# Attention and a gated layer on one core: three pairs of transposes cut into 64-row halves, an earlier release of the weight loads, and a new order of the instructions

## The chip, the core and the metric

The kernel runs on one core of a Trainium2 chip. The core has five engines that each work through a queue of their own: TensorE (PE; its weight loads are listed as PEld), VectorE (DVE), ScalarE (ACT), GpSimd (POOL) and SyncE (SP), which here only issues transfers (DMAs). Engines wait for each other through semaphores. The metric is the time of one execution on the device in microseconds (us); lower is better.

## The reference

The input `x` has 2048 rows of 448 features. Two layers follow each other, each on a normalized copy of its input and added to it:

```
xn  = layernorm(x)
q, k, v = split(xn @ wqkv)                 # 16 heads of 28
phi(t)  = [softmax(t @ w_phi), softmax(-t @ w_phi)]          # per head, 56 features
kv = phi(k)^T v ;  z = sum over rows of phi(k)               # per head, over all 2048 rows
o  = phi(q) kv / (phi(q) z + 1e-6)
h  = x + o @ wo
hn = layernorm(h)
out = h + (sigmoid(hn @ w_gate) * (hn @ w_up)) @ w_down      # 1792 inner features
```

All tensors are bf16. `kv` and `z` need every row before the first row of `o` can be made.

## The kernel before

**Tiles and stages.** The 2048 rows are 16 tiles of 128, in four chunks of four tiles. First stage: per tile `t` the statistics (`bst`, `agg`, `pow1`, `nm1`), the normalized tile `xn`, its transpose `xT` (features on partitions), then the projections. `Wk` and `Wq` are folded with `w_phi` first (`wT`, `w2m`, `w2e`). Tiles 0 to 3 are projected in pairs (`vv` for v, `pp` for the k features), tiles 4 to 15 one by one (`pva`, `pvb`, which make both). From a tile's projections come the copy of v (`v1`), two exponentials (`ek`), their sums and reciprocals (`ss`, `rs`), the features `phi`, and the kv product `kva`, `kvb`, summed in PSUM over all tiles. `pq` makes the q features of a chunk, `eq` their exponentials. Second stage: `kvz` takes the kv sums out of PSUM, and per tile `num` multiplies, `rsm qq b c rden o` divide (in `o` the tile is ready), `oT` transposes, `woa`/`wob` project, and `h` adds the residual. Third stage: layernorm of `h` (`nm sq ve pow2 hn`, for tiles 0 and 1 `bs2 ag2 pow2 hn`), its transpose `hT`, the gate and up matmuls (`ga`, `gb`), the sigmoid (`sig`) and the product (`hh`), the down matmuls (`dn`, `dp`, `dm`, `dl`), the last addition (`fin`) and `out`. Names end in the tile, or in the first tile and a part.

**64-row halves.** The 448 features of a contraction are laid out so that every matmul uses only 64 rows of the array, and two matmuls, on the upper and the lower 64 rows, run side by side into two PSUM banks (`pair` and `both`, L304 to L325, which call the matmul at L309). The second half of such a pair (`pvb`, `ppb`, `gb`...) exchanges the banks of the first, so each bank is written from the other half of the array; `op` is told which half writes which bank (`half`), and where that changes (`crosses`, L74) PE waits for its own earlier matmuls.

**Transposes.** Those of `xT4` to `xT15`, and of `oT` and `hT` from tile 2 on, are transposing transfers issued by SP (L583, L823, L856). The first ones, `xT0` to `xT3`, `oT0 oT1`, `hT0 hT1`, are made on PE by `pe_transpose` (L533): four transposes of 128 x 128 with all 128 rows into one bank, and one copy out of it by ACT or DVE (`evac`, L529), whose name ends in `e` (`xT2e`). `oT0` and `hT0` are called by `otrans` (L817) and `htrans` (L859).

**What sets the order.** `ORDER` (L223) lists every instruction group by name for each of the five queues; the engine on which a name stands is the engine that does it, where a choice exists. `Graph` (L19) keeps for each tile of memory who wrote and read it last and emits the waits. Two names, `wwo` and `wgu`, emit nothing but waits on PE: for the loads of `wo`, and for those of the gate and up weights. `PACE` (L289) adds one wait to SP's queue: the load `ld_wg1` waits for a kv product; all later loads and transposing transfers are queued behind it. The waits that the prediction speaks of: `ppa2` (tiles 2 and 3) needs both transposes, and its banks emptied by `ek0` and `ek1`; `pva4` needs `v1_2` and `ek2`; `pqa2_1` needs the banks of `pqa1_1` emptied by two `eq`; `num2` and later products write the banks that `c` of the tile before reads; `woa0` needs both `oT` and the banks they were copied from; `ga0_2` needs both `hT`, and `ga0_0` the bank that `eq3_1` empties.

Of the kernel before, what the change touches and what calls it, by code (L numbers as in the profile page):

```python
# [18 lines left out]
class Graph:  # L19
# [90 lines left out]
    def emit(self, nc):  # L110
# [85 lines left out]
P = 128  # L196
# [92 lines left out]
PACE = {"ld_wg1": "kva14"}  # L289
# [36 lines left out]
def build(nc, A_x, A_wqkv, A_w_phi, A_wo, B_w_gate, B_w_up, B_w_down, out):  # L326
# [10 lines left out]
    with ExitStack() as es:  # L337
# [71 lines left out]
        def B(i):  # L409
            return ("bank", i)  # L410
# [121 lines left out]

        def pe_transpose(name, srcs, bank, dst, rkey, wkey):  # L533
            ps = bk16(bank)[:, 0:512]

            def f(e):
                for kt, src in enumerate(srcs):
                    p = e.transpose(ps[:, kt * P:(kt + 1) * P], src, ident[:])  # L538
# [25 lines left out]
        def xnorm(t, a):  # L564
# [14 lines left out]
            if t < 4:  # L579
                pe_transpose("xT%d" % t, [xn_pad[:, s, kt * P:(kt + 1) * P] for kt in range(KT)], 6 + t % 2,  # L580
                             xnT[0][:, :, TS(t)], ("xn", s), ("xnT", t))
            else:
                op("sp", "xT%d" % t, lambda e: e.dma_start_transpose(out=xnT[t // 4][:, :, TS(t)], in_=xn_pad[:, s, :]),  # L583
                   r=[("xn", s)], w=[("xnT", t)], dma="tr", nring=64)
# [67 lines left out]
        def proj(t):  # L652
            bp, bv = t % 2, 2 + t % 2
            pairop("pva%d" % t, "pvb%d" % t, pair(bk(bp)[:, 0:D], bk(bv)[:, 0:D], x(t), x(t), wk2, wv),
                   [("xnT", t)] + W2k + wv_keys, bp, bv)

        def proj2(nm, t, b, w, r):
            pairop("%sa%d" % (nm, t), "%sb%d" % (nm, t), pair(bk(b)[:, 0:D], bk(b + 1)[:, 0:D], x(t), x(t + 1), w, w),
                   [("xnT", t), ("xnT", t + 1)] + r, b, b + 1)
# [51 lines left out]
        def pq(c, i, b):  # L711
# [3 lines left out]
            r = W2q + [("xnT", 4 * c + j) for j in range(4)]  # L715
# [101 lines left out]
        def otrans(t):  # L817
            so = t % NO
            if t < 2:
                pe_transpose("oT%d" % t, [o_pad[:, so, kt * P:(kt + 1) * P] for kt in range(KT)], 2 + t % 2, oT[:, so, :, :],  # L820
                             ("opad", so), ("oT", so))
            else:
                op("sp", "oT%d" % t, lambda e: e.dma_start_transpose(out=oT[:, so, :, :], in_=o_pad[:, so, :]),  # L823
                   r=[("opad", so)], w=[("oT", so)], dma="tr", nring=64)

        def resid(t, b, ha=False):
# [28 lines left out]
            if t >= 2:  # L855
                op("sp", "hT%d" % t, lambda e: e.dma_start_transpose(out=hnT[c][:, :, TS(t)], in_=hn_pad[:, s, :]),  # L856
                   r=[("hn", s)], w=[("xnT", t)], dma="tr", nring=64)

        def htrans(t):  # L859
            s = t % NH  # L860
            pe_transpose("hT%d" % t, [hn_pad[:, s, kt * P:(kt + 1) * P] for kt in range(KT)], t, hnT[0][:, :, TS(t)], ("hn", s), ("xnT", t))

        def wout(t):
# [14 lines left out]
            r = [("oT", t % NO), ("oT", (t + 1) % NO)] + wo_keys + ([("x", t), ("x", t + 1), "ident"] if ha else [])  # L878
# [5 lines left out]
        def wout1(t):  # L884
# [5 lines left out]
            r = [("oT", so)] + wo_keys  # L890
# [10 lines left out]
        def gate_up(t0, n, ff):  # L901
# [3 lines left out]
            hk = [("xnT", t) for t in range(t0, t0 + n)]  # L905
# [129 lines left out]
```

## Time and profile before

| | us |
|---|---|
| median of 3 runs | 202.55 |
| the three runs | 202.16 to 202.61 |
| the profiled execution, its own time | 202.7 |
| its span in the profile | 200.8 |
| PE busy in the span | 195.5 |
| DVE busy | 132.0 |
| ACT busy | 89.4 |
| POOL busy | 56.2 |

The profile is one execution; times in it start with its span, which leaves out 1.9 us around it. "Busy" of PE includes the tail of every matmul, so a busy PE can still be standing between two starts; starts in the timeline show that better. The page's chain goes back from the last instruction to what released it each time. In the timeline a row gives start, length, engine, line and operation, what is written and read, how many instructions are merged in it, and in brackets how long the engine had stood and for whom. Because a helper records all paired matmuls, their line is L309 for all of them, and they are told apart by what they read: `Wk`/`wv_sb` with `xnT` is `pva`/`pvb`, `Wq` is `pq`, `v,phi` is a kv product, `kvz,eq` is `num`, `wg_sb`/`wu_sb` is `ga`/`gb`, `wo_e`/`wo_o` is `woa`/`wob`. L538 is a transpose on PE, L612 a fold (`w2m`), L671/L672 are the two exponentials of `ek`, L721 one of `eq`.

### The profile page before, as it was taken

How to read it: one execution, taken by the hardware profiler on the slowest of the kernel's cores; microseconds unless marked ns; L12 is line 12 of the kernel's file. 1: busy time of each engine (PE TensorE's matmuls, PEld its weight loads, DVE VectorE, ACT ScalarE, POOL GpSimd, SP SyncE). 2: the span in 40 equal slices, each digit the busy share in tenths (PEclk: the TensorE clock that was granted, in tenths of full speed). 3: DMA queues.
4: the chain of work that ended last, by engine and by line, in shares of the span. 5: the costliest groups of instructions: out<-in, count | busy, mean ns of one | idle time of the engine just before them, and what ended most of it. 6: DMA issues, size and time to landing. Idle time of an engine off the chain costs nothing.

```text
span 200.8 us, 5854 instructions
## 1 busy us (share of the span) xinstructions
PE 195.5 (97%) x2516; PEld 114.4 (57%) x2516; DVE 132.0 (66%) x308; ACT 89.4 (45%) x174; POOL 56.2 (28%) x95
## 2 busy tenths in 40 slices
PE   7999999999999999999999999999999999999995
PEld 4835556565568778787444444555555555554443
DVE  5999999978888986576569877346332422272224
ACT  2668988898883451434232432324323212222220
POOL 5779948633343207510170110001400000000000
PEclk9999999999999999999999999999999999999999
DMA  6965346749984230360015220020312000004002
GB/s 157 316 140 129 54 83 76 221 144 302 309 206 66 52 57 15 66 82 3 0 29 124 56 42 10 20 58 26 65 38 52 0 3 2 0 3 137 0 3 91
DMA packets 32490, 16.26 MB, mean 81 GB/s; under 512 B 24720, under 2 KB 31568, under 8 KB 32464
## 3 DMA queue, kind: packets, MB, share of 16 engines
q1 hardware_dynamic: 32336, 15.86, 33.7%
q8 instruction: 20, 0.33, 0.7%
q14 instruction: 6, 0.05, 0.1%
q10 hardware_dynamic: 128, 0.03, 0.1%
HBM read 8.34 MB, written 1.84 MB: 51 GB/s over the span
## 4 chain that ended last, share of the span: by engine, by line
PE 92%; ACT 3%; DMA 2%; issue 1%; SPq 1%; DVE 0%
PE psum L309 84%; PE psum L954 5%; DMA wk_sb<-in_A_wqkv_dram 2%; ACT hhT L671 1%; ACT eq L721 1%; ACT hhT L672 1%; PE psum L524 1%; PE psum L538 1%; PE psum L612 1%; SPq L413 1%; PE psum L599 0%; ACT xnT L531 0%; ACT v L531 0%; DVE x_sb L961 0%
## 5 line engine op out<-in xcount | busy, mean ns | idle before, releaser
L309 PE MATMUL psum<-xnT,wu_sb 64*128 64x512 bf16 (+1 forms) x490 | 93.6, 333 | 0.0
L309 PE MATMUL psum<-xnT,wg_sb 64*128 64x512 bf16 (+1 forms) x490 | 93.5, 333 | 0.1
L925 ACT ACTIVATE sg_sb<-psum 128x512 bf16<-128x512 f32 x56 | 33.2, 596 | 90.1 <-PE psum L309 89.5
L926 DVE SCALAR_TENSOR_TENSOR hhT<-sg_sb,psum 128x512 bf16<-128x512 bf16 x56 | 37.7, 684 | 52.1 <-ACT sg_sb L925 51.7
L309 PEld LDWEIGHTS psum<-xnT,wg_sb 64*128 64x128 bf16 x490 | 44.6, 94 | 20.9 <-DVE hhT L926 2.5
L309 PEld LDWEIGHTS psum<-xnT,wu_sb 64*128 64x128 bf16 x490 | 44.7, 94 | 13.9
L309 PE MATMUL psum<-wd_sb,hhT 64*128 64x448 bf16 x336 | 37.3, 349 | 0.0
L309 PEld LDWEIGHTS psum<-wd_sb,hhT 64*128 64x128 bf16 x336 | 17.8, 94 | 14.2 <-DVE x_sb L836 0.5
L309 PE MATMUL psum<-Wk,xnT 64*128 64x448 bf16 x112 | 22.2, 350 | 0.5 <-ACT hhT L672 0.2
L309 PE MATMUL psum<-wv_sb,xnT 64*128 64x448 bf16 x112 | 22.3, 351 | 0.1
L810 POOL TENSOR_TENSOR o_pad<-c_sb,rden 128x448 bf16<-128x448 bf16 x11 | 10.2, 935 | 28.5 <-DVE rden L806 28.4
L675 DVE TENSOR_REDUCE ss<-hhT 128x32 f32<-128x896 bf16 x16 | 16.8, 1060 | 0.2 <-ACT hhT L672 0.2
L721 ACT ACTIVATE eq<-psum 120x1024 bf16<-120x1024 f32 x16 | 15.6, 1030 | 0.6 <-PE psum L309 0.4
L685 POOL TENSOR_TENSOR phi<-hhT,rs 128x896 bf16<-128x896 bf16 x8 | 13.6, 1710 | 5.6 <-DVE rs L681 3.4
L309 PE MATMUL psum<-xnT,Wq 64*120 64x512 bf16 x112 | 14.8, 383 | 0.3 <-ACT eq L721 0.2
L845 POOL TENSOR_SCALAR ve<-ssq 128x1 f32<-128x1 f32 x11 | 2.2, 201 | 41.8 <-ACT junk L842 41.5
L309 PE MATMUL psum<-wo_o,oT 64*128 64x448 bf16 x56 | 13.2, 350 | 0.0
L309 PE MATMUL psum<-wo_e,oT 64*128 64x448 bf16 x56 | 13.2, 349 | 0.0
L961 DVE SCALAR_TENSOR_TENSOR x_sb<-psum,x_sb 128x448 bf16<-128x448 f32 (+2 forms) x17 | 9.4, 592 | 2.9 <-PE psum L954 1.6
L954 PE MATMUL psum<-wd_sb,hhT 128*128 128x448 bf16 (+2 forms) x70 | 11.2, 316 | 0.0
L309 PEld LDWEIGHTS psum<-Wk,xnT 64*128 64x128 bf16 x112 | 7.8, 94 | 5.8 <-PE psum L309 1.0
L671 ACT ACTIVATE hhT<-psum 128x448 bf16<-128x448 f32 x16 | 8.8, 553 | 4.4 <-PE psum L309 4.2
(105 smaller groups left out, 234.4 us busy)
## 6 DMA issues: line engine op xcount, KB each, us to landing
out_dram<-x_sb SPq DMA_DIRECT2D x15, 112.0 KB, 1.8
x_sb<-in_A_x_dram SPq DMA_DIRECT2D x7, 224.0 KB, 4.2
wd_sb<-in_B_w_down_dram SPq DMA_DIRECT2D x7, 224.0 KB, 5.1
wg_sb<-in_B_w_gate_dram SPq DMA_DIRECT2D x3, 448.0 KB, 5.8
wu_sb<-in_B_w_up_dram SPq DMA_DIRECT2D x3, 448.0 KB, 5.7
wv_sb<-in_A_wqkv_dram SPq DMA_DIRECT2D x2, 224.0 KB, 4.7
wk_sb<-in_A_wqkv_dram SPq DMA_DIRECT2D x2, 196.0 KB, 4.1
wo_e<-in_A_wo_dram SPq DMA_DIRECT2D x1, 336.0 KB, 3.3
```

The lines of the kernel that those rows point to most:

```text
L309: p = e.matmul(o, lhsT=w, rhs=r, start=st, stop=sp, tile_position=(row, 0))
L413: return op(eng, name, lambda e: e.dma_start(dst, src), r=r, w=w, dma="in" if eng == "sp" else "ain", nring=48 if eng == "sp" else 8, kb=kb)
L671: e.activation(ek[:, s, :, 0, :], src, ACT.Exp)
L675: op("dve", "ss%d" % t, lambda e: e.tensor_reduce(ss[:, s, :].rearrange("p (b h) -> p b h", h=2), eks.rearrange("p b (d h) -> p b h d", h= ...
L685: return e.tensor_tensor(phi[:, sp, :, :, :].rearrange("p b a n -> p (b a) n")[:, :, 0:56].rearrange("p b (d h) -> p b d h", h=2), eks.rea ...
L721: op("act", "eq%d_%d%s" % (c, i, "pm"[sg]), lambda e, sg=sg: e.activation(eq[c][:, sg, 2 * i:2 * i + 2, :].rearrange("p g n -> p (g n)"), ...
L810: return e.tensor_tensor(o_pad[:, t % NO, off:off + D].rearrange("p (h d) -> p h d", h=H), c_sb[:, t % NS, :, 0:DH], rden[:, t % NS, :][:, ...
L845: op(("pool", "dve"), "ve%d" % t, lambda e: e.tensor_scalar(ve2[:, t:t + 1], ssq2[:, t:t + 1], 1.0 / D ** 3, EPS, op0=ALU.mult, op1=ALU.ad ...
L925: op("act", "sig" + nm, lambda e: e.activation(sg_sb[:, k, 0:W], bk(bg)[:, 0:W], ACT.Tanh, scale=0.5), r=[B(bg)], w=[("sg", k)])
L926: op("dve", "hh" + nm, lambda e: e.scalar_tensor_tensor(out=dst, in0=sg_sb[:, k, 0:W].rearrange("p (f n) -> p f n", n=N), scalar=1.0, in1= ...
L954: p = e.matmul(bk(b)[:, lo:hi], lhsT=hb[:, ff, TS(t)], rhs=wd_sb[:, ff, lo:hi], start=ff == 0, stop=ff == FT - 1)
L961: op("dve", "fin%d%s" % (t, nm), lambda e: e.scalar_tensor_tensor(out=h_sb[:, t, lo:hi], in0=bk(b)[:, lo:hi], scalar=0.5, in1=h_sb[:, t, l ...
```

## The change

Three pairs of PE transposes (`xT2 xT3`, `oT0 oT1`, `hT0 hT1`) become one group each, made by a new helper: every 128 x 128 transpose is cut into its upper and lower 64 rows, at the row halves 0 and 64 of the array, like the matmuls around it. The upper halves of both tiles go to one bank and the lower halves to the other, and one copy per bank writes that half of both tiles:

```
+        def pair_transpose(names, srcs, banks, dst, rkeys, wkeys):
+            ps = [bk16(b)[:, 0:512] for b in banks]
+
+            def f(e):
+                for i, tile in enumerate(srcs):
+                    for kt, src in enumerate(tile):
+                        o = slice((i * KT + kt) * 64, (i * KT + kt + 1) * 64)
+                        for h, rows in enumerate((LO, HI)):
+                            p = e.transpose(ps[h][:, o], src[rows], ident[rows, rows], tile_position=(64 * h, 0))
+                return p
+            op("pe", names[0], f, r=["ident"] + rkeys, w=[B(b) for b in banks], rows=64, half={b: h for h, b in enumerate(banks)})
+            for h in range(2):
+                evac(names[h] + "e", dst[h], ps[h].rearrange("p (t k s) -> p t k s", t=2, k=KT), B(banks[h]), [k[h] for k in wkeys])
...
-            if t < 4:
+            if t in (2, 3):
...
-PACE = {"ld_wg1": "kva14"}
+PACE = {"ld_wg1": "kva12"}
```

So a reader of either tile waits for both copies. `otrans` and `htrans` call the helper once, for tiles 0 and 1 together. The release of `ld_wg1` and of what SP has behind it moves from the kv product of tile 14 to that of tile 12.

The four orders of ACT, PE, DVE and POOL are new (SP's is the same). Where the prediction speaks of them, first as before and then as after:

```
PE   ppa0 ppb0 warm9 xT2 xT3 vva0 vvb0 ppa2 ppb2 vva2 seed vvb2 w2m1_0 w2m1_1 kva0 pva4 kvb0 pvb4 pva5 w2m1_2 w2m1_3 pvb5
     ppa0 warm9 ppb0 vva0 xT2 vvb0 ppa2 seed ppb2 vva2 w2m1_1 vvb2 w2m1_0 w2m1_3 kva0 pva4 pvb4 pva5 kvb0 kva1 pvb5 w2m1_2
PE   qs pqa1_1 num0 num1 pqb1_1 pqa2_0 num2 pqb2_0 pqa2_1 oT0 oT1 num3 pqb2_1 woa0 wob0 pqa3_0 num4
     qs pqa1_1 num0 pqb1_1 num1 pqa2_0 num2 pqb2_0 pqa2_1 oT0 pqb2_1 num3 woa0 wob0 pqa3_0 wgu num4
PE   pqb3_0 pqa3_1 pqb3_1 num5 hT1 hT0 woa2 ga0_2 ga0_0 ga0_1 num6
     pqb3_0 pqa3_1 pqb3_1 num5 hT0 woa2 ga0_2 ga0_0 ga0_1 num6
PE   woa4 num8 wob4 ga0_8 ga0_9 ga0_10 gb0_8 gb0_9 woa6 ga0_11 wob6 gb0_10 ga0_12 gb0_11 ga0_13 dn0_0 dn0_4 gb0_12 gb0_13 num9
     woa4 num8 wob4 ga0_8 ga0_9 ga0_10 ga0_11 gb0_8 gb0_9 gb0_10 woa6 num9 wob6 ga0_12 ga0_13 gb0_11 wwo gb0_12 gb0_13 dn0_0 dn0_4 dn0_8
ACT  w2e0_2 par ek0 xT3e ek1 v1_0 v1_1 nm1_6 ek2 ek3 v1_2
     w2e0_2 nm1_4 par ek0 ek1 v1_1 nm1_6 v1_0 ek2 w2e1_1 v1_2 ek3
ACT  eq1_0p kvzA kvzB eq1_0m eq1_1p eq1_1m eq2_0m oT0e eq2_0p eq2_1m eq2_1p h1 h0 eq3_0p eq3_0m eq3_1p eq3_1m
     eq1_0m kvzB kvzA eq1_0p eq1_1m eq1_1p eq2_0p oT1e oT0e eq2_0m eq2_1p eq2_1m h0 h1 eq3_0m eq3_0p eq3_1p eq3_1m
DVE  bst4 xn2 agg5 agg4 agg7 bst6 xT2e agg6 ss0
     bst4 agg5 agg4 agg7 xn2 bst6 bst9 xT3e xT2e agg6 ss0
DVE  c1 rsm2 rden1 qq2 b2 c2 oT1e rsm3 rden2
     c1 rsm2 rden1 qq2 o1 b2 c2 rden2 rsm3
DVE  o7 hh0_4 ve3 hh0_6 h4 nm2 h5 nm3 rsm8 hn2 hn3 qq8 hh0_8 h6 h7 b8 c8 rden8
     o7 hh0_4 hh0_6 rsm8 qq8 h5 h4 b8 c8 nm4 rden8 hh0_8 h6 h7
POOL o4 o5 o6 ve2 pow2_2 pow2_3 ve5
     o4 o5 o6 nm3 nm2 ve2 pow2_2 hn2 ve3 pow2_3 hn3 ve4
```

`phi5` and `phi11` move from DVE to POOL and `phi10` the other way, `v1_13` from DVE to ACT, `o1` from POOL to DVE. From `ga4_1` (the gate matmuls of the second chunk) on, PE's order is the same as before but for `dp2_0`, one place earlier, and the moved `wgu`.

More of the change, by code (lines that the diff above doesn't have):

```diff
@@ L578, in xnorm @@
             op(("act", "dve", "pool"), "xn%d" % t, (fa, fd, fp), r=[("x", t), ("rst1", a), need], w=[("xn", s)])
-            if t < 4:
+            if t in (2, 3):
+                if t == 3:
+                    v = xnT[0][:, :, 2 * P:4 * P].rearrange("p k (t h s) -> p h t k s", t=2, h=2)
+                    pair_transpose(("xT2", "xT3"), [[xn_pad[:, u % NX, kt * P:(kt + 1) * P] for kt in range(KT)] for u in (2, 3)], (6, 7),
+                                   [v[:, 0], v[:, 1]], [("xn", 2 % NX), ("xn", 3 % NX)], [XT(2), XT(3)])
+            elif t < 2:
                 pe_transpose("xT%d" % t, [xn_pad[:, s, kt * P:(kt + 1) * P] for kt in range(KT)], 6 + t % 2,
-                             xnT[0][:, :, TS(t)], ("xn", s), ("xnT", t))
+                             xnT[0][:, :, TS(t)], ("xn", s), XT(t))
             else:
                 op("sp", "xT%d" % t, lambda e: e.dma_start_transpose(out=xnT[t // 4][:, :, TS(t)], in_=xn_pad[:, s, :]),
-                   r=[("xn", s)], w=[("xnT", t)], dma="tr", nring=64)
+                   r=[("xn", s)], w=[XT(t)], dma="tr", nring=64)
         for ts in ([0], [1], [2], [3], [4, 5], [6, 7], [8, 9, 10, 11], [12, 13, 14, 15]):
@@ L714, in pq @@
                           lambda h, k: xnT[c][h, k, :], lambda h, k: xnT[c][h, k, :])
-            r = W2q + [("xnT", 4 * c + j) for j in range(4)]
+            r = W2q + [XT(4 * c + j) for j in range(4)]
             op("pe", "pqa%d_%d" % (c, i), f1, r=r, w=[B(b), B(b + 1)], rows=64, half={b: 0, b + 1: 1})
@@ L819, in otrans @@
             if t < 2:
-                pe_transpose("oT%d" % t, [o_pad[:, so, kt * P:(kt + 1) * P] for kt in range(KT)], 2 + t % 2, oT[:, so, :, :],
-                             ("opad", so), ("oT", so))
+                if t == 1:
+                    v = oT[:, 0:2, :, :].rearrange("p t k (h s) -> p h t k s", h=2)
+                    pair_transpose(("oT0", "oT1"), [[o_pad[:, u, kt * P:(kt + 1) * P] for kt in range(KT)] for u in (0, 1)], (2, 3),
+                                   [v[:, 0], v[:, 1]], [("opad", 0), ("opad", 1)], [OT(0), OT(1)])
             else:
                 op("sp", "oT%d" % t, lambda e: e.dma_start_transpose(out=oT[:, so, :, :], in_=o_pad[:, so, :]),
-                   r=[("opad", so)], w=[("oT", so)], dma="tr", nring=64)
+                   r=[("opad", so)], w=[OT(so)], dma="tr", nring=64)
         def resid(t, b, ha=False):
@@ L856, in resid @@
                 op("sp", "hT%d" % t, lambda e: e.dma_start_transpose(out=hnT[c][:, :, TS(t)], in_=hn_pad[:, s, :]),
-                   r=[("hn", s)], w=[("xnT", t)], dma="tr", nring=64)
+                   r=[("hn", s)], w=[XT(t)], dma="tr", nring=64)
         def htrans(t):
-            s = t % NH
-            pe_transpose("hT%d" % t, [hn_pad[:, s, kt * P:(kt + 1) * P] for kt in range(KT)], t, hnT[0][:, :, TS(t)], ("hn", s), ("xnT", t))
+            if t == 1:
+                v = hnT[0][:, :, 0:2 * P].rearrange("p k (t h s) -> p h t k s", t=2, h=2)
+                pair_transpose(("hT0", "hT1"), [[hn_pad[:, u, kt * P:(kt + 1) * P] for kt in range(KT)] for u in (0, 1)], (0, 1),
+                               [v[:, 0], v[:, 1]], [("hn", 0), ("hn", 1)], [XT(0), XT(1)])
         def wout(t):
@@ L877, in fb @@
                             xp(t, 2, HI, False) + [(bk(2)[:, 0:D], ot(t)(HI, k), wo_e[HI, k, :], False, k == 2) for k in (0, 1, 2)])
-            r = [("oT", t % NO), ("oT", (t + 1) % NO)] + wo_keys + ([("x", t), ("x", t + 1), "ident"] if ha else [])
+            r = [OT(t % NO), OT((t + 1) % NO)] + wo_keys + ([("x", t), ("x", t + 1), "ident"] if ha else [])
             op("pe", "woa%d" % t, fa, r=r, w=[B(2), B(3)], rows=64, half={2: 0, 3: 1})
@@ L889, in part @@
                 return [(bk(b)[:, 0:D], oT[h, so, k, :], w[h, k, :], first and k == ks[0], not first and k == ks[-1]) for k in ks]
[L890 removed]
+            r = [OT(so)] + wo_keys
             op("pe", "woa%d" % t, lambda e: both(e, part(LO, lo, True), []), r=r, w=[B(b)], rows=64, half={b: 0})
@@ L904, in gate_up @@
             ns = slice((t0 % 4) * P, (t0 % 4) * P + N)
-            hk = [("xnT", t) for t in range(t0, t0 + n)]
+            hk = [XT(t) for t in range(t0, t0 + n)]
             two = n == 2
```

8 lines of the change are left out of this document (6 added, 2 removed), and 64 rows, old and new, of the table ORDER.

## The prediction

> **What bounds the kernel now.** I read the page first: busy shares, the slices, and the chain that ended last.
>
> ```profile
> span 200.8 us, 5854 instructions
> PE 195.5 (97%) x2516; PEld 114.4 (57%) x2516; DVE 132.0 (66%) x308; ACT 89.4 (45%) x174; POOL 56.2 (28%) x95
> ...
> PEclk9999999999999999999999999999999999999999
> ...
> PE 92%; ACT 3%; DMA 2%; issue 1%; SPq 1%; DVE 0%
> ```
>
> TensorE (PE) holds 92% of the chain, at full granted clock in every slice. The change adds no matmul columns, so the answer lies in the small rest: where PE stands. For that I read the same chain in order of time (start, length, what).
>
> ```profile
> 10.55 0.76 PE psum L309 x6
> ...
> 11.34 0.54 ACT hhT L671
> 11.88 0.43 ACT hhT L672
> 12.32 0.48 ACT xnT L531
> 12.79 0.45 ACT hhT L671
> 13.24 0.45 ACT hhT L672
> ...
> 13.82 0.95 PE psum L309 x8
> ...
> 18.02 2.49 PE psum L309 x30
> 20.52 0.50 PE psum L612 x8
> ...
> 47.20 1.95 ACT eq L721 x2
> ...
> 58.21 65.46 PE psum L309 x960
> ```
>
> The reader is to see two things. ACT sets the pace from 11.34 to 13.69 (`ek0`, the copy `xT3e`, `ek1`) and from 47.20 to 49.15 (`eq1_1p`, `eq1_1m`). From 58.21 on the chain is PE for 65 us without a break: whatever PE wins before that point is kept, if nothing new stops it later. Times below are on the axis of this execution; an earlier start is written as a shift.
>
> **Part 1: the transposes themselves.** Rows of the PE timeline, from `num0` to `num3`:
>
> ```profile
> 45.86 0.63 PE L309 MATMUL psum<-kvz,eq 56*128 56x60 bf16 x32
> 46.31 1.72 PE L309 MATMUL psum<-xnT,Wq 64*120 64x512 bf16 x14
> ...
> 49.19 1.07 PE L309 MATMUL psum<-xnT,Wq 64*120 64x512 bf16 x8 [0.25 <-ACT eq L721]
> 50.20 0.62 PE L538 MATMUL psum<-ident,o_pad 128*128 128x128 bf16 x8
> 50.75 0.40 PE L309 MATMUL psum<-kvz,eq 56*128 56x60 bf16 x16
> ```
>
> Eight 128-row transposes (`oT0 oT1`) hold PE from 50.20 to 50.75, 0.55 us. Some 0.1 of it is the switch back to 64-row work, and I put as much for the switch ahead of 50.20 (an estimate: the row shows only its sum with the matmuls). The new pair has 16 pieces of 64 columns, in two row halves side by side, without a switch. The nearest row is 32 matmuls of 60 columns from 45.86 to 46.31: 14 ns apart, so 16 take 0.23. A pair saves 0.55 + 0.1 - 0.23 = 0.42, and three pairs 1.26. That is the naive sum. I don't forecast it, because at all three places PE stands for something else just before or behind. Bounds for a pair: -0.42 if the halves overlap as in that row, -0.20 if they don't (16 x 28 ns = 0.45).
>
> The Trainium skill ("TensorE: Matmul & The Clock Gate", Part 1, under "Wait — 56ns, not 53.3ns?") speaks against small pieces: starts of matmuls are never closer than about 25 ns, however few columns they have. By it a pair would take 16 x 25 = 0.40 us and save 0.25. The row above has 14 ns over both halves together, so the measurement decides here, and the floor can hold at most for one half by itself.
>
> **Part 2: the start, to `pva4`.** In the chain above `ek0`, `xT3e`, `ek1` follow on ACT and `ppa2` starts at 13.82, when `ek1` has emptied its bank. The change moves `xT3e` to VectorE (DVE): 0.48 leaves ACT's chain. Into ACT's queue comes `nm1_4`, with `par` and `ek0` queued behind its wait for `agg4` and `agg5`, which DVE now does before `xn2`.
>
> ```profile
> 10.63 0.40 DVE L573 TENSOR_SCALAR xn_pad<-x_sb,mv,rst 128x512 bf16<-128x512 bf16 x1
> 10.95 0.33 DVE L546 BATCH_NORM_AGGREGATE mv<-st 128x2 f32<-128x9 f32 x3
> ...
> 11.78 0.42 DVE L531 COPY xnT<-psum 128x512 bf16<-128x512 bf16 x1
> ```
>
> Moved ahead of `xn2` the three aggregates end near 10.95, so `nm1_4` is done by 11.2, and `ek0`, which waits for `ppb0` until 11.31, loses nothing. `ppb0` itself comes 0.06 later, since `warm9` with two switches now stands between `ppa0` and `ppb0`. So `ek1` ends at 13.69 - 0.48 + 0.06 = 13.27. The other input of `ppa2` is the pair's copies, both on DVE: the pair runs behind `vva0` at about 11.95, and two copies of 0.42 end near 13.15. ACT stays last: `ppa2` at 13.40, -0.42. `pva4` (18.02) keeps that: its releasers `ek2` and `v1_2` follow PE, and `v1_2` has one Wq copy ahead of it in place of `ek3`. Bounds: 0 (if the copies, in a DVE queue that is full here, come last) and -0.60.
>
> **Part 3: tiles 4 to 15, to the kv sums.** PE is full here but for small stands between `pva` and `pvb`, which exchange banks:
>
> ```profile
> 26.26 0.28 PE L309 MATMUL psum<-v,phi 64*128 64x58 bf16 x8
> 26.49 0.36 PE L309 MATMUL psum<-wv_sb,xnT 64*128 64x448 bf16 x1
> ...
> 30.18 0.39 PE L309 MATMUL psum<-v,phi 64*128 64x58 bf16 x16
> 30.41 0.36 PE L309 MATMUL psum<-wv_sb,xnT 64*128 64x448 bf16 x1
> ```
>
> Between the start of the kv products and the first `pvb` matmul lie 0.23 us, whether one product (8 matmuls, half of it) or two (16) are put there: one leaves 0.12 unused, two nothing. Before, six tiles have one (4, 8, 9, 11, 13, 14). After, five have one (6, 8, 9, 11, 14) and one has none (`pva4 pvb4`): -0.12 + 0.23. `w2m1_3`, nearly half of the 0.50 at 20.52, leaves this stretch for the one before, where ACT is last: -0.21. Sum -0.10. DVE gives `phi5` to POOL and `v1_13` to ACT and takes only `xT3e`, so its chain to `phi15` gets shorter; ACT comes within about 0.1 of PE at tiles 9, 13 and 15. Bounds -0.3 and +0.4.
>
> **Part 4: from the kv sums to the first gate matmul.** Between `num0` and `pqb1_1` nothing is left (`num1` moves behind), so `pqb1_1` starts half of the 0.45 from 45.86 to 46.31 earlier, -0.22, and with it the two exponentials at 47.20 and `pqa2_1`, which stood 0.25 for them at 49.19. That is where PE wins. Then:
>
> ```profile
> 48.47 1.83 POOL L810 TENSOR_TENSOR o_pad<-c_sb,rden 128x448 bf16<-128x448 bf16 x2 [6.24 <-DVE rden L806]
> ...
> L810 DVE TENSOR_TENSOR o_pad<-c_sb,rden 128x448 bf16<-128x448 bf16 x5 | 3.1, 625 | 0.1
> ...
> 50.63 0.58 ACT L531 COPY oT<-psum 128x512 bf16<-128x512 bf16 x1 [0.58 <-PE psum L538]
> 51.11 2.86 ACT L721 ACTIVATE eq<-psum 120x1024 bf16<-120x1024 f32 x3
> ...
> 55.60 3.77 ACT L721 ACTIVATE eq<-psum 120x1024 bf16<-120x1024 f32 x4
> ```
>
> `o1` leaves GpSimd (POOL), where it ended at 50.30, for DVE, where it ends near 49.85. The oT pair needs both tiles: 49.9 to 50.3 with its tail. Its two copies are both on ACT, 50.35 to 51.4, so `woa0` starts near 51.5, 0.17 earlier than before. Behind these copies stand `eq2_0m eq2_1p eq2_1m`, three as at 51.11; they end near 54.2 and hold nobody. On DVE `o1` pushes `c2` and so `num3` back by 0.5, still ahead of `woa0`. `h0 h1` and the four exponentials at 55.60 follow `woa0`: they end at 59.20 instead of 59.37 and free the bank of `ga0_0` so much sooner. The hT pair can't go before its own banks are free, near 57.35 by the second of these four; its copies end at 58.7, early enough. So its 0.42 is lost into a stand of PE, and part 4 is -0.17. Bounds +0.3 and -0.5.
>
> The pause: `ld_wg1` waits for `kva12` instead of `kva14`, some 2 us sooner; behind it on SP stand the other weight loads, `oT2` and `oT3`, in the same order as before. `wgu` (all gate and up weights) is now asked for behind `pqa3_0`, near 54.3 (53.8 with the shifts).
>
> ```profile
> 46.33 0.44 SPq L413 DMA_DIRECT2D wu_sb<-in_B_w_up_dram  x1
> ...
> DMA to landing us min/median/max: 8.0/8.0/8.0
> ```
>
> The last of them landed at 46.33 + 8.0 = 54.3. Issued 2 us sooner it lands near 52: worth nothing, and costing 0.5 if it didn't come sooner.
>
> **Part 5: behind 59 us.** PE's work is the same, in another order, and the end follows it. The tightest place is `num9`, moved up to stand right behind `woa6`: it needs `c8`.
>
> ```profile
> 69.89 0.64 DVE L851 TENSOR_SCALAR hn_pad<-x_sb,nm,rst 128x512 bf16<-128x512 bf16 x2
> ...
> 73.71 0.64 DVE L804 TENSOR_TENSOR c_sb<-b_sb,psum 128x464 bf16<-128x464 bf16 x1
> ...
> 69.98 0.35 PE L309 MATMUL psum<-wo_e,oT 64*128 64x448 bf16 x1
> ```
>
> `c8` ended at 74.35. Now `hn2 hn3` (0.64) and `ve3 nm2 nm3` (small) go to POOL, where `ve` and `pow2` stand ahead of them and the transposing transfers `hT2 hT3` behind, and `hh0_8 h6 h7` go behind `c8`: `hn2 hn3` ended at 70.53, and that less about 1, plus `qq8` and `b8` and `c8` at 0.64 each, is 70.9 to 71.2. PE gets there with `woa6` (69.98), pushed back by a few more gate products, near 71.4. DVE is again just in time at `ga2_4` and `ga2_10`. For some hundredths here and there I put +0.10.
>
> **Sum.** -0.42 - 0.10 - 0.17 + 0.10 = -0.59. The profiled execution took 202.7 (span 200.8 and 1.9 around it), so it would take 202.1; the median of the three runs is 202.55, 0.15 lower, and from it comes 201.96, I say 202.0.
>
> **Rivals.**
> (a) *Slower: oT3 lands late.* `o3` is made 0.5 later than before on the axis of part 4 (`c2`, `num3`, `c3` behind `o1`), which eats the shift: `oT3` is issued at 54.3 by the clock as before, while `woa2`, behind the hT pair, now asks at 57.2 (57.7 less 0.5). How long these transfers took, `oT2 oT3`, `oT4 oT5`, and the ten later ones:
>
> ```profile
> DMA to landing us min/median/max: 2.9/3.6/4.2
> ...
> DMA to landing us min/median/max: 4.2/4.3/4.4
> ...
> DMA to landing us min/median/max: 2.4/2.5/3.2
> ```
>
> At 2.5 it lands at 56.8 and all is well; PE stands behind `woa2` until the hT copies are done, so the point is a landing after 3.3. At 4.2 it lands at 58.5, `woa2` runs to 59.3, and `ga0_0` starts at 59.8, where it started at 59.44: 202.55 + 0.4 + 0.1 = 203.05. For it: three of the first four took over 4. Against it: weights were in flight beside those, and these now land some 2 us sooner.
> (b) *No change: DVE and ACT eat the start.* If the copies, or ACT's queue at tiles 9 to 15, take 0.4 back, PE stands there instead: 202.5.
> (c) *The halves don't overlap.* 0.22 more per pair; the hT copies then end near 58.9 and part 4 gives nothing: 202.55 - 0.42 + 0 = 202.1 to 202.2. By the skill's floor it would be this case too.
>
> **How the numbers follow.** Forecast 0.47, (a) 0.20, (b) 0.23, (c) 0.10. A measurement of this kernel tells about 0.2% (0.4 us) from no change. Of the forecast 0.40 falls under 202.15, and half of (c): faster 0.45. Of (a) most lies over 202.95, with a little of (b): slower 0.21. Same 0.34. The range goes down to parts 2 and 4 at their low ends (0.18 and 0.33 further), 201.4, and up to (a) with a little of part 3, 203.2.
>
> **What would show it.** After the change: `ppa2` near 13.4 and `pva4` near 17.6; the 16 pieces of a pair in 0.23 us with no stand at the switches; `ga0_0` near 58.8 (59.44 less parts 2 to 4); no wait of PE over 0.1 from there to 123 us. Wrong would be: `ppa2` behind a copy on DVE, a stand ahead of `woa2` (a), or at `num9`, `ga2_4` or `ga2_10` for DVE.

## The result and the profile after

| | before | after |
|---|---|---|
| median, us (5 runs of each, beside each other) | 202.27 | 203.93 |
| lowest to highest | 202.10 to 202.61 | 203.62 to 204.66 |
| span of the profiled execution | 200.8 | 201.8 |

The ratio is 1.0075, with a 95% interval of 1.0058 to 1.0091. The changed kernel is slower; 202.0 was forecast, with 203.2 as the upper end. Here and below a ratio leaves out the few executions that lie over 1.5% above the fastest of their kernel, while medians and ranges are of all. The page of the changed kernel, in the lines that the prediction shows of the kernel before, and with its two instruction queues:

```profile
span 201.8 us, 5901 instructions
...
PE 195.8 (97%) x2540; PEld 111.5 (55%) x2540; DVE 134.3 (67%) x308; ACT 90.7 (45%) x175; POOL 54.2 (27%) x94
...
PEclk9999999999999999999999999999999999999999
...
q8 instruction: 20, 0.33, 0.7%
q14 instruction: 6, 0.05, 0.1%
...
PE 74%; DVE 16%; POOL 2%; ACT 2%; DMA 2%; issue 1%; SPq 1%; DVEq 0%
```

PE is as busy as before and at full granted clock, but its share of the chain fell from 92% to 74%, and DVE's rose from 0 to 16%. One row plays no part in the prediction: the queue `q8 instruction`, which is code on its way from memory. It has 20 transfers of 16 KB, while PE has 5080 matmuls and weight loads, so one per some 254 of them; these are taken for PE's blocks of code. The queue `q14` moves code in pieces of 8 KB, six in the whole span. Both will matter. The chain in order of time (start, length, what):

```profile
26.13 1.78 DVE xn_pad L593
27.91 1.99 DVE ss L700 x2
30.26 0.63 DVE phi L710
31.23 1.69 POOL phi L710
...
33.78 1.70 POOL phi L710
35.52 6.24 PE psum L309 x120
...
59.07 12.04 PE psum L309 x230
71.10 0.68 issue
71.78 52.93 PE psum L309 x694
```

Two things are new in it. Up to 35.52 the chain runs over DVE (from 6.69 on, ahead of the lines shown) and then POOL, with one `xn` of 1.78 us in it; and PE's long stretch, unbroken before from 58.21 on, has a hole of 0.68 at 71.10. PE's timeline shows what stands behind them (a bracket gives how long PE stood and for whom):

```profile
11.61 0.40 PE L547 MATMUL psum<-ident,xn_pad 64*128 64x64 bf16 x16
11.85 0.74 PE L309 MATMUL psum<-wv_sb,xnT 64*128 64x448 bf16 x6
12.97 0.93 PE L309 MATMUL psum<-Wk,xnT 64*128 64x448 bf16 x8 [0.39 <-ACT hhT L697]
...
32.45 0.36 PE L309 MATMUL psum<-Wk,xnT 64*128 64x448 bf16 x1 [0.28 <-DMA xnT<-xn_pad]
...
35.52 0.26 PE L309 MATMUL psum<-v,phi 64*128 64x58 bf16 x6 [0.26 <-POOL phi L710]
...
50.21 0.41 PE L547 MATMUL psum<-ident,o_pad 64*128 64x64 bf16 x16
50.44 0.85 PE L309 MATMUL psum<-xnT,Wq 64*120 64x512 bf16 x6
...
71.78 0.35 PE L309 MATMUL psum<-wo_e,oT 64*128 64x448 bf16 x1 [0.68 <-issue]
```

The rows at 32.45, 35.52 and 71.78 are `pva12` (waits for the transfer `xT12`), `kva8` (waits for `phi8` on POOL) and `woa6` (its releaser isn't shown; below it will be `oT7`). Counted from start to start of PE's groups, with the usual distance taken off, they stood about 0.45, 0.45 and 0.85. The whole span by stretches of PE:

| stretch | before | after | difference | forecast |
|---|---|---|---|---|
| to `ppa0` | 9.56 | 9.20 | -0.37 | none |
| `ppa0` to `pva4` | 8.46 | 7.96 | -0.50 | -0.42 |
| `pva4` to the kv sums (`qs`) | 26.27 | 27.25 | +0.98 | -0.10 |
| `qs` to `ga0_0` | 15.15 | 15.23 | +0.08 | -0.17 |
| `ga0_0` to the end | 141.35 | 142.16 | +0.81 | +0.10 |

The first row is no work of the change: in the profiles of this study `ppa0` starts anywhere between 9.15 and 9.82, whatever the kernel, with the landing of the first loads. The two profiled executions lie 1.0 us apart, the medians 1.7: the changed kernel's is the fastest of its five, and that of before took 202.7, so the table shows only a part of the loss.

**Two theories.** *Theory 1, for the third stretch:* `phi5`, moved to POOL, stops DVE. Both kernels around `xn12` (start, length, engine), first the one before, then the changed one:

```profile
25.64 1.01 POOL L554 TENSOR_TENSOR rst<-mv,neghalf 128x4 f32<-128x4 f32 x1 [0.23 <-DVE mv L546]
25.70 0.32 DVE L573 TENSOR_SCALAR xn_pad<-x_sb,mv,rst 128x512 bf16<-128x512 bf16 x1
...
27.13 0.77 POOL L576 TENSOR_SCALAR xn_pad<-x_sb,nm,rst 128x512 bf16<-128x512 bf16 x1 [0.49 <-ACT hhT L672]
27.18 0.87 DVE L573 TENSOR_SCALAR xn_pad<-x_sb,mv,rst 128x512 bf16<-128x512 bf16 x1 [0.16 <-issue]
```

```profile
26.07 1.69 POOL L710 TENSOR_TENSOR phi<-hhT,rs 128x896 bf16<-128x896 bf16 x1 [0.46 <-DVE rs L706]
26.13 1.78 DVE L593 TENSOR_SCALAR xn_pad<-x_sb,mv,rst 128x512 bf16<-128x512 bf16 x1 [0.20 <-issue]
```

The same DVE instruction takes 0.32 us at 25.70 in the kernel before. In the changed one `xn12` starts 0.06 behind POOL's `phi5` and ends 0.15 behind it; before, it started 0.05 behind POOL's `xn13` and ended 0.15 behind that. The Trainium skill ("SBUF — State Buffer", "Who interferes with whom") says that DVE and GpSimd share a pair of memory ports as an exclusive lock, that a `tensor_scalar` in its two-port mode needs it, and that whichever comes second is blocked until the first is done. The rows with `xn13` and `phi5` agree with that; the row at 25.70, undisturbed beside POOL's 1.01 us on 4 elements a row, shows that not every instruction of POOL's blocks.

*Theory 2, for the last stretch:* a transposing transfer lands late if a 16-KB block of instructions is fetched while it is in flight, and the change moves the blocks. The DMA view, cut to the flight of `oT7` (issue to landing, us), before and after:

```profile
oT<-o_pad SPq DMA_TRANSPOSE x1, 2.4
```

```profile
q8 instruction: 1, 0.02, 1.4%
...
oT<-o_pad SPq DMA_TRANSPOSE x1, 4.1
```

Before, no block was fetched in that window; the ninth came at 70.92, behind the landing at 69.80, and fell into the flight of `hT2`, which took 3.18 and for which nobody waited. After, the ninth comes at 69.67, 2.1 after the issue of `oT7` (67.58), which lands at 71.69, and `woa6` starts at 71.78. A transpose in 64-row halves has 16 matmuls per pair in place of 8, and each brings a weight load: 16 more PE instructions per pair, 48 in all. Each block is therefore asked for earlier in the code. *The rivals:* that the new order or the early release of the weights makes the transfers late, that transposing transfers delay each other when several are in flight, or that the pair transposes are slow of themselves.

### The profile page after: what moved, and what is told of

Read it like the earlier page. It is cut to its first block, busy times and chain, and to the rows that moved or that the text cites. A ratio compares the mean times of both kernels' runs of the same rounds, so it can differ in the third digit from the quotient of the medians.

```text
span 201.8 us, 5901 instructions
## 1 busy us (share of the span) xinstructions
PE 195.8 (97%) x2540; PEld 111.5 (55%) x2540; DVE 134.3 (67%) x308; ACT 90.7 (45%) x175; POOL 54.2 (27%) x94
## 4 chain that ended last, share of the span: by engine, by line
PE 74%; DVE 16%; POOL 2%; ACT 2%; DMA 2%; issue 1%; SPq 1%; DVEq 0%
PE psum L309 68%; PE psum L983 5%; DVE ss L700 4%; DVE st L565 4%; DMA x_sb<-in_A_x_dram 2%; POOL phi L710 2%; ACT eq L746 1%; DVE c_sb L829 1%; DVE xn_pad L593 1%; DVE phi L710 1%; DVE xnT L531 1%; DVE rs L706 1%; DVE b_sb L826 1%; SPq L413 1%; ACT kvz L779 1%
## 5 line engine op out<-in xcount | busy, mean ns | idle before, releaser
L309 PEld LDWEIGHTS psum<-wd_sb,hhT 64*128 64x128 bf16 x336 | 17.3, 94 | 14.5 <-DVE x_sb L863 0.5
L835 POOL TENSOR_TENSOR o_pad<-c_sb,rden 128x448 bf16<-128x448 bf16 x8 | 7.5, 937 | 34.5 <-DVE rden L831 29.9
L710 POOL TENSOR_TENSOR phi<-hhT,rs 128x896 bf16<-128x896 bf16 x9 | 15.4, 1711 | 3.7 <-DVE rs L706 2.7
L826 DVE TENSOR_TENSOR b_sb<-psum,qq 128x464 bf16<-128x464 f32 x16 | 10.2, 635 | 0.7 <-PE psum L309 0.5
```

Source lines behind the costliest of these rows:

```text
L309: p = e.matmul(o, lhsT=w, rhs=r, start=st, stop=sp, tile_position=(row, 0))
L710: return e.tensor_tensor(phi[:, sp, :, :, :].rearrange("p b a n -> p (b a) n")[:, :, 0:56].rearrange("p b (d h) -> p b d h", h=2), eks.rea ...
L826: op("dve", "b%d" % t, lambda e: e.tensor_tensor(h3(b_sb), OMv[:, :, :, 0:EV], h2(qq)[:, :, :, None].to_broadcast([P, NB, 8, EV]), ALU.mul ...
L835: return e.tensor_tensor(o_pad[:, t % NO, off:off + D].rearrange("p (h d) -> p h d", h=H), c_sb[:, t % NS, :, 0:DH], rden[:, t % NS, :][:, ...
```

## The experiments

The kernel before was run beside each of them; ratios are to it.

**`phi5` back on VectorE, the rest as changed.**

```
-POOL  pow1_12 phi5 xn13        DVE  rs5 xn12 ss6
+POOL  pow1_12 xn13             DVE  rs5 xn12 phi5 ss6
```

> The changed kernel with one name moved: phi5 goes back from GpSimd to VectorE. Theory 1 (GpSimd's phi5 held VectorE's xn12: 1.78 us instead of some 0.35, and everything behind it on VectorE came late): xn12 under 0.9 us, the stands of PE ahead of kva8 (0.45) and pva12 (0.46) shrink to under 0.2 together, the kv sums are done near 43.8 instead of 44.57, total 0.4 to 0.9 us under the changed kernel: 203.0 to 203.5. Theory 2 (late transposing transfers alone): xT12 and oT7 stay late, total within 0.3 of 203.9.

Measured: 202.96 (202.83 to 203.56), ratio 1.0032 (1.0019 to 1.0044), against 1.0075 with `phi5` on POOL. Its DVE timeline, and the DMA view over the flight of `oT7`:

```profile
26.31 0.41 DVE L593 TENSOR_SCALAR xn_pad<-x_sb,mv,rst 128x512 bf16<-128x512 bf16 x1 [0.21 <-issue]
26.64 0.62 DVE L710 TENSOR_TENSOR phi<-hhT,rs 128x896 bf16<-128x896 bf16 x1
```

```profile
q8 instruction: 1, 0.02, 1.5%
...
oT<-o_pad SPq DMA_TRANSPOSE x1, 4.0
```

`xn12` and `phi5` together now take 1.0 us on DVE where `xn12` alone took 1.78, the stands ahead of `pva12` and `kva8` are gone, and `pva4` to `qs` is 26.46 instead of 27.25. `oT7` is late as before, `woa6` stands 0.71.

**34 PE instructions fewer ahead of everything** (the warm-up's columns in 17 fewer, larger matmuls), once on the changed kernel, once with `phi5` on VectorE as well.

```
-(6, 128), (4, 128), (6, 128), (8, 128)
+(2, 384), (1, 512), (2, 384), (2, 512)
```

> The changed kernel with 17 fewer warm-up matmuls of the same total number of columns, so 34 fewer PE instructions ahead of everything. Theory 2 (a transposing transfer is late when a 16 KB block of the instruction queue is fetched while it is on its way, and a block is fetched every 256 PE instructions): all fetches come some 34 instructions later, the one at 69.7 us near 70.5, oT7 lands 2.5 us after its issue instead of 4.1, the stand of PE ahead of woa6 (0.85) goes to under 0.1, total 0.6 to 0.9 under the changed kernel: 203.0 to 203.3; other transfers may get late instead. Theory 1: nothing changes, 203.6 to 204.1.

> The changed kernel with phi5 back on VectorE and with the 17 fewer warm-up matmuls. If theories 1 and 2 each explain a part, the gains add: 1.2 to 1.7 under the changed kernel, 202.2 to 202.7. If only one holds, it is no better than the better of the two single edits by over 0.2.

Measured: 205.73 (204.32 to 207.40), ratio 1.0141 (1.0081 to 1.0201), and 205.14 (203.62 to 205.32), ratio 1.0118 (1.0079 to 1.0158). In both `oT7` lands in time and `woa6` doesn't stand, as theory 2 has it. But something else came up, in PE's timeline of the first:

```profile
51.26 0.30 PE L309 MATMUL psum<-kvz,eq 56*128 56x60 bf16 x9 [2.50 <-issue]
```

PE stops for 2.50 us (1.70 in the second) in the middle of `num2`, between two matmuls of one group that wait for nothing in the program, and in both kernels at the same place in the code. The fifth block was fetched only at 48.66 (46.49 in the second), where the changed kernel had it at 42.72: it seems to have queued behind the weight loads, of which the first run issued the first two at 38 to 40 us and the rest from 41.5 on. That PE stopped for want of instructions is what fits; that the weights held the block up is argued from the times only. Behind the stand of 2.50 PE ran slow besides: the granted clock was 0.50 in each us from 52 to 55, and 1.00 again from 56 on. Behind the one of 1.70 it stayed at 1.00. Neither profiled execution is typical of its kernel: the first took 206.74, between 204.32 and 207.40, the second 203.62, the other three 205.00 to 205.32. So this pair of runs says nothing of the total, and the count has to be shifted less, or elsewhere.

**The three pair transposes alone**, in the orders and with the release of before.

```
 the changed kernel, with before's ORDER and PACE but for:
-warm9 xT2 xT3 vva0      pqa2_1 oT0 oT1 num3      num5 hT1 hT0 woa2
+warm9 xT2 vva0          pqa2_1 oT0 num3          num5 hT0 woa2
```

> The kernel before with the three pairs of half-row transposes alone, in the old order (each pair where the second of its two transposes stood last), old release of the loads. If each pair's 0.42 us counted in full, 1.26 us under the kernel before: 201.0. By the reasoning of the prediction (PE stands for ACT's and VectorE's work at these places) 0.1 to 0.4 under: 201.9 to 202.2. If waiting for both tiles costs more than the pieces save (the oT pair waits for o1, the hT pair for eq3_0's bank), 202.3 to 202.8.

Measured: 204.80 (204.54 to 205.77), ratio 1.0134 (1.0104 to 1.0165). PE's timeline at `woa2` and `woa6`:

```profile
58.55 0.35 PE L309 MATMUL psum<-wo_e,oT 64*128 64x448 bf16 x1 [1.04 <-DMA oT<-o_pad]
...
71.94 0.35 PE L309 MATMUL psum<-wo_e,oT 64*128 64x448 bf16 x1 [1.51 <-issue]
```

The pieces themselves take the forecast 0.22 to 0.24 us per pair. What costs is late transfers: `oT2` landed 5.81 after its issue (weight loads in flight, and a block at 55.78), `oT3` behind it at 58.41, and `oT7` 4.19 after its issue (a block at 69.54). `woa2` needs `oT2` and `oT3`; here, and in the runs below in which it stands, it starts 0.13 to 0.14 behind the landing of `oT3`. Alone the pair transposes make this kernel 2.4 us slower, and yet they are no slower on PE. The next two runs say whether that is the instruction count.

**48 more PE instructions in the kernel before, and nothing else.**

```
-(4, 512), ... (6, 128), (4, 128), ... (2, 128)
+(16, 128), ... (12, 64), (8, 64), ... (4, 64)
```

> The kernel before, with 24 more matmuls in the warm-up (the same columns in smaller pieces), that is 48 more TensorE instructions, as many as the three half-row pair transposes add, and nothing else. Theory 2: the ninth block is fetched at about 69.3 us instead of 70.9, within oT7's flight (67.4 to 69.8), so oT7 lands about 4 us after its issue and woa6 stands about 1 us; the third at about 28.6 lies in xT12's flight; 203.0 to 204.2 in all. The rival (the instruction count means nothing; the pair transposes cost time through what they do): 202.2 to 202.5, as before, and oT7 2.4 us after its issue.

Measured: 205.24 (204.83 to 207.35), ratio 1.0156 (1.0101 to 1.0210): more even than theory 2 expected. No transpose, order or release was touched. The profiled execution is the longest of the four, about 2 us over the next, so its stands below are more than the median's. PE at `woa2` and `woa6`, and the DMA view over `oT7`:

```profile
61.61 0.35 PE L309 MATMUL psum<-wo_e,oT 64*128 64x448 bf16 x1 [1.33 <-DMA oT<-o_pad]
...
74.75 0.35 PE L309 MATMUL psum<-wo_e,oT 64*128 64x448 bf16 x1 [1.26 <-issue]
```

```profile
q8 instruction: 1, 0.02, 1.5%
...
oT<-o_pad SPq DMA_TRANSPOSE x1, 3.9
```

The rival (the count means nothing) is out. The same two groups stand as with the pairs alone; another 0.8 went ahead of `pva11`, for `xT11`, 5.09 us from issue to landing, and as much ahead of `kva8`, for a `phi` on POOL.

**The pair transposes alone, with 38 PE instructions taken off the warm-up.**

```
-(2, 128), ... (6, 128), (4, 128), (6, 128), (8, 128), (2, 128)
+(1, 256), ... (2, 384), (1, 512), (2, 384), (2, 512), (1, 256)
```

> The three pair transposes in the order of before, as in the run with them alone (204.8), but with 19 matmuls fewer in the warm-up (the same columns in larger pieces): 10 TensorE instructions more than before instead of 48 behind the last pair. Theory 2: the seventh and the ninth block come at about 58.5 and 70.5 us instead of 55.8 and 69.5, oT2 and oT7 land on time, the stands ahead of woa2 (1.23) and woa6 (1.68) go, 201.9 to 202.6. The rival (the pair transposes are slow of themselves, in their evacuations or in what they hold up): 204.5 to 205.

Measured: 202.30 (202.01 to 203.17), ratio 0.9995 (0.9980 to 1.0011). All 2.4 us are back, by nothing but fewer, larger matmuls ahead of the real work:

```profile
58.52 0.35 PE L309 MATMUL psum<-wo_e,oT 64*128 64x448 bf16 x1 [0.36 <-DMA oT<-o_pad]
...
70.24 0.35 PE L309 MATMUL psum<-wo_e,oT 64*128 64x448 bf16 x1
```

```profile
oT<-o_pad SPq DMA_TRANSPOSE x1, 2.4
```

`woa6` follows without a stand, as expected. `woa2` does not: it still stands 0.36. `oT2` took 5.11 and `oT3` 3.87 with no block in their flight, beside weight loads alone, so at this place the block is only a part of the lateness. From `qs` to `ga0_0` this kernel took 15.18, with that stand in it, against 15.15 before: what the halves save there is lost again. They are not slow; nor are they a gain that can be measured.

**`phi5` on VectorE and 130 PE instructions more.**

```
-(4, 512), (1, 512), (1, 128), (2, 128), (1, 128), (6, 128), (4, 128), (6, 128), (8, 128), (2, 128)
+(32, 64), (8, 64), (2, 64), (4, 64), (2, 64), (12, 64), (8, 64), (12, 64), (16, 64), (4, 64)
```

> The changed kernel with phi5 back on VectorE, and with its warm-up matmuls cut into pieces of 64 columns: 65 matmuls more, the same columns, so 130 more TensorE instructions (a matmul and its weight load each) before the first projection. Theory 2 (a 16-KB block of TensorE instructions that is fetched while a transposing transfer is in flight makes that transfer land late): every block comes 130 instructions earlier in the code; the ninth, fetched at 68.9 us with phi5 on VectorE, comes at about 65.3, during oT6 instead of oT7; oT7 lands about 2.4 us after its issue instead of 3.98, woa6 does not stand (0.71 before), and the time falls from 202.96 to about 202.3 (202.0 to 202.7), if the sixth block, which would now come at about 46 us among the weight loads, does not starve TensorE. The rival (oT7 is late because of the order of the transfers, not because of the fetch): oT7 late as before, woa6 standing, 202.9 to 203.2.

Measured: 202.09 to 207.05, ratio 1.0022 (0.9995 to 1.0049). The median of 203.27 lies in a gap: of ten executions five took 202.1 to 202.7, as theory 2 expected, three 203.9 to 204.1 and two 207. So the time decides nothing. The profiled execution is one of the slower ones (204.10). In it the ninth block came at 66.93, ahead of `oT7`, which took 2.43 us, and `woa6` didn't stand: that half of the expectation held. What it lost elsewhere is first of all a transfer at `pva4`:

```profile
18.07 0.36 PE L309 MATMUL psum<-Wk,xnT 64*128 64x448 bf16 x1 [0.85 <-DMA xnT<-xn_pad]
```

`xT4` landed 5.12 after its issue at 12.9; the loads of `x` were still in flight, and a block was fetched at 15.37. Which of the two did it isn't separated. PE also stood 0.41 ahead of a kv product, for a `phi` on POOL, and 0.52 inside a `num`, for nothing that the profile names.

**`phi5` on VectorE, weights released at `kva14` as before.**

```
-PACE = {"ld_wg1": "kva12"}
+PACE = {"ld_wg1": "kva14"}
```

> The changed kernel with phi5 back on VectorE, and the weight loads from ld_wg1 on held to kva14, as before, instead of kva12: what the earlier release is worth. ld_wg1 issues at about 43 instead of 40.4 us, ld_wd2 lands at about 56 instead of 54.2, oT2 at about 56.8 instead of 54.8. If that transfer is in time either way, 202.8 to 203.2 against 202.96; if the earlier release carries the pair of hT0 and woa2, about 203.4 to 204.

Measured: 204.22 (203.12 to 204.66), ratio 1.0079 (1.0056 to 1.0102), so here the earlier release carries about 1 us (the difference of the ratios; 1.3 by the medians). PE at `woa2`, and the DMA view over the issue of `oT2`:

```profile
58.97 0.35 PE L309 MATMUL psum<-wo_e,oT 64*128 64x448 bf16 x1 [0.67 <-DMA oT<-o_pad]
```

```profile
oT<-o_pad SPq DMA_TRANSPOSE x1, 6.0
```

With the release at `kva12` `oT2` took 2.80 and was down at 54.76, `oT3` at 57.19, ahead of `woa2`'s need; with it at `kva14` weights and a block (55.90) lay in the flight of `oT2`, `oT3` was down only at 58.83, and `woa6` stood 0.97 besides.

**The same release in the kernel before** (`kva14` to `kva12`, nothing else):

> The kernel before with the weight loads from ld_wg1 on held to kva12 instead of kva14, nothing else. On the changed kernel the same edit undone cost 1.26 us, because oT2 then landed 6.03 us after its issue, behind the weights and a block of instructions fetched at 55.9 us. If the release has a worth of its own, the time falls by 0.3 to 1 us, 201.4 to 202.1. If it only decides which transfers a block of instructions meets (theory 2), then in the kernel before, where woa2 does not stand and no block is fetched between 52 and 58 us, it gives nothing: 202.2 to 202.6, with oT2 landing about 1 to 2 us earlier all the same; later than that only if the fifth block, 43.2 us, now queues behind the weights and TensorE starves in num1 or num2.

Measured: 202.37 (202.11 to 202.81), ratio 0.9985 (0.9968 to 1.0001). `oT2` landed at 55.96 instead of 56.84, and nobody had waited for it. The release has no worth of its own that this can tell; it only matters where a late transfer is on PE's path.

**`phi5` alone moved to POOL in the kernel before.**

```
-POOL  pow1_12 xn13             DVE  ss7 phi5 phi6
+POOL  pow1_12 phi5 xn13        DVE  ss7 phi6
```

> The kernel before with phi5 alone moved from VectorE to GpSimd, ahead of xn13 there. Theory 1 (VectorE's xn12 cannot run while GpSimd runs a phi): phi5 runs on GpSimd from about 26.6 to 28.3 us, xn12 (starts about 27.2, 0.87 us before) ends only behind it, 1.3 to 1.5 us, xn13 on GpSimd 1.2 us later; xT12 and xT13 land 0.6 us later and the time rises to 202.7 to 203.3. The rival (phi5's engine does not matter, xn12 was long in the changed kernel for another reason): xn12 at most 0.9 us, 202.3 to 202.5.

Measured: 202.20 (202.11 to 203.50), ratio 0.9998 (0.9983 to 1.0014). The lock is there, the cost isn't:

```profile
26.23 1.69 POOL L685 TENSOR_TENSOR phi<-hhT,rs 128x896 bf16<-128x896 bf16 x1
26.79 1.27 DVE L573 TENSOR_SCALAR xn_pad<-x_sb,mv,rst 128x512 bf16<-128x512 bf16 x1 [0.17 <-issue]
```

`xn12` again ends 0.15 behind `phi5`, at 28.06. That is 10.42 behind `pva4`, 0.4 later than before (10.03), though DVE is rid of `phi5`'s 0.6. `xT12`, issued then, met a block at 30.07, took 4.15 and landed at 32.24; `pva12` started at 32.36, as far behind `pva4` as before and without a stand. So the old order had room for the delay, and theory 1 has to be narrowed: `phi5` on POOL costs by its place in the new orders, where `xn12` starts beside it and nearly all of its 1.69 us is lost to DVE. In the changed kernel `xT12` was then issued at 27.94 with a block following at 29.09, and landed 4.46 later; with `phi5` on VectorE it was issued at 26.76 and down at 29.18, just as the block came. Part of what theory 1 explains went through theory 2.

**`phi5` on VectorE and 20 PE instructions fewer.**

```
-(2, 128), ... (6, 128), ... (6, 128), ... (2, 128)
+(1, 256), ... (2, 384), ... (2, 384), ... (1, 256)
```

> The changed kernel with phi5 on VectorE and 10 matmuls fewer in the warm-up (same columns), 20 TensorE instructions fewer. Theory 2: the ninth block moves from 68.9 to about 69.5 us, just behind the landing that oT7 has undisturbed (69.35), so woa6's stand of 0.71 goes: 202.2 to 202.6 against 202.96. Its danger: the fifth block moves from 42.8 to 43.2 us or later, further into the weight loads; if it queues behind them as with 34 instructions fewer, TensorE stops in num2 and the time is 203.5 to 205. The rival (the count of instructions does nothing to oT7): woa6 stands as before, 202.8 to 203.1.

Measured: 202.61 (201.88 to 203.19), ratio 1.0002 (0.9985 to 1.0020), against 1.0032 with them. The ninth block came at 69.52, 2.4 behind the issue of `oT7`, and `woa6` doesn't stand. The block fell into the flight of `hT2` instead, which took 3.83 and for which nobody waited:

```profile
oT<-o_pad SPq DMA_TRANSPOSE x1, 2.4
```

The fifth block came at 43.48 and PE did not run dry. `woa2` stood 0.29 for `oT3`, down at 57.88.

**`phi5` on VectorE, `oT` and `hT` transposed whole again.**

```
-                if t == 1:
-                    pair_transpose(("oT0", "oT1"), ...)
+                pe_transpose("oT%d" % t, ...)
 and the same for hT0 and hT1
```

> The changed kernel with phi5 on VectorE, and the pairs oT0/oT1 and hT0/hT1 transposed whole again as before (xT2/xT3 stays a pair): 32 TensorE instructions fewer, 16 of them ahead of the seventh block, all ahead of the ninth. Each pair costs up to 0.3 us more on TensorE (0.55 against 0.23). Theory 2: the ninth block comes at about 69.7 behind oT7's landing, woa6's stand of 0.71 goes, 202.5 to 203.0 in all, so that the halves are worth nothing here. The rival (halves are a gain by themselves, blocks do not matter): the stand stays and the time rises by up to 0.6, 203.2 to 203.6.

Measured: 202.89 (202.13 to 203.34), ratio 1.0012 (0.9991 to 1.0033). `oT7` is in time (2.42) with the ninth block at 70.20. PE stood 0.50 once, at 47.61 inside a `num`, for nothing that the profile names. Two of the three pairs can be taken out without a loss that the intervals show.

**All transfers together.** From the traces of the two kernels and all twelve runs, the transposing transfers issued after 65 us, where no weights are in flight (but for one run, in which the last landed at 67.01). Undisturbed they take 2.4 to 2.57 us from issue to landing; late means over 2.9. Each is sorted by when a block of instructions (of PE or another engine) began to be fetched, counted from its issue; transfers with two blocks near are in none of the rows from the second on:

| block begins | transfers | late | longest |
|---|---|---|---|
| none from 0.9 ahead to 2.4 behind the issue | 197 | 0 | 2.57 |
| 0.8 ahead to 0 | 17 | 8 | 3.46 |
| 0 to 2.0 behind | 72 | 55 | 4.29 |
| 2.0 to 2.4 behind | 33 | 7 | 4.53 |

No transfer of this stretch was late without a block near its flight. It is PE's blocks of 16 KB that count. In the third row they are 56 of the 72, and 55 of these 56 transfers were late; the 16 with just an 8-KB piece of `q14` were all in time (2.69 at most), as were the 9 such in the last row. (Two transfers with such a piece 2.0 and PE's block 2.9 to 3.0 behind their issue took 3.4.) Nor do transposing transfers make each other late: of the 197 in the first row 187 had another one in flight.

## Why the prediction was wrong

**What cost what.** Of the 0.75%, 0.43 is `phi5`'s place (1.0075 to 1.0032) and 0.30 the count of PE instructions, by the stand at `woa6` (1.0032 to 1.0002; the two intervals just touch, at 1.0019 and 1.0020). What is left of the change is 1.0002 (0.9985 to 1.0020): neither the 0.3% gain that I forecast nor a loss.

**Part 1** held in size: 16 pieces took 0.23 to 0.24 us, with no stand at the switches, so rival (c) did not happen. The starts lie 14 ns apart over both halves and some 28 ns within one, so the floor of about 25 ns between starts that the Trainium skill ("TensorE: Matmul & The Clock Gate", Part 1) gives can hold within a half at most. Part 1 failed in what it counted: it counted the pieces' time and not that they are 48 instructions more. By the pairs alone (1.0134) and with the count restored (0.9995), that was the dearest thing in the diff.

**Part 2** held: `ppa0` to `pva4` -0.50 for a forecast -0.42, and `ppa2` waits for ACT, as the bracket at 12.97 says. (That `ppa2` came at 12.97 and not 13.40 is mostly the earlier `ppa0`.) It is the order's gain and not the halves': with the pairs alone in the old order the stretch took 8.46, as before.

**Part 3** is the step that failed first: "DVE gives `phi5` to POOL ... so its chain to `phi15` gets shorter". It became longer, since `xn12` beside `phi5` took 1.78. The trace of the kernel before did hold the warning: `xn12` took 0.87 beside POOL's `xn13`, and such an instruction 0.32 to 0.40 elsewhere. With `phi5` put back the stretch is still +0.19 against a forecast -0.10. Of that 0.3, 0.19 is a stand ahead of `pva13` (at 33.91 in that run), where the kv product that stood there before has moved away: `pva13` starts 0.14 behind the end of `v1_11` on ACT, which empties its bank. The forecast had ACT within about 0.1 of PE there; it comes last. The other 0.1 stays open.

**Part 4** came out at +0.08 for -0.17. The gain at `pqa2_1` came, but `o1` ended on DVE only at 50.06, where 49.85 was forecast, and the pair went at 50.21 and not at 49.9. Of both differences 0.12 is the later `qs` of this execution (44.41 against 44.29). The rest is some 0.1 at `o1`, since the small operations ahead of it were left out of my sum, and 0.1 more from its end to the pair. The `wgu` wait cost nothing and no stand was seen ahead of `woa2`: rival (a) didn't happen at its place. The early release, which I priced at nothing, is worth nothing alone (0.9985), but beside the new block times it keeps `oT2` and `oT3` out of a loss of about 1 us (1.0079 to 1.0032).

**Part 5** is the second failed step: "+0.10" for everything behind 59 us took each of the later transfers at its usual 2.4 to 2.5 us, though the prediction's own row of them goes up to 3.2. `oT7` took 4.1 and cost 0.85. Rival (a) had the right kind of event, a transposing transfer of 4.2 us, but named the weights as its cause and `oT3` as its place. Its event came in other runs: with the pairs alone, with 48 instructions more and with the release at `kva14`, `woa2` did stand for `oT3`. The Trainium skill ("Runtime: NRT & Kernel Launch", "Instruction fetch mechanics") describes blocks of 16 KiB with 256 instructions that each engine fetches through a DMA queue of its own, and calls the cost mostly hidden. Size and number agree with the 20 packets here; hidden it is not in this kernel.

## What to carry to other kernels

Count the instructions that an edit adds, not only their time: where code streams in by blocks, it moves every later fetch, and a transfer with a known usual duration has a second one that applies when a block falls into its flight. So a small difference between two orders may be luck of alignment; add or take away a few dozen harmless instructions before you believe in it. When work moves to GpSimd, name the VectorE instruction that will run beside it, and look in the trace for a row where that kind already took twice its usual time.

## What the runs showed of the hardware that was not expected

- A transposing transfer of 128 rows takes 2.4 to 2.57 us undisturbed and up to 4.5 with a 16-KB block of PE's instructions fetched in its flight (table above). An 8-KB piece of the queue `q14` alone made none late. Beside weight loads `oT2` took up to 5.1 without a block, and 5.8 to 6.4 in three runs with one.
- TensorE stood 2.50 us in the middle of a group, at the same place of the code in two kernels (1.70 in the other), when the fifth block came at 48.66 and 46.49 us in place of 42.7. Behind the stand of 2.50 the granted clock was 0.50 for some 3 us.
- 48 extra small matmul and weight load instructions in the warm-up, where PE has nothing else to do, made the kernel 1.56% slower.
- Sixteen transposes of 64 rows and 64 columns, in two halves, take 0.23 us, 14 ns apart.
